# Top-32 attention and a mixture of experts on one core: the last key chunk of the outputs on 64 columns per head

## The chip, the core and the metric

The kernel runs on one core of one Trainium2 chip. The metric is device time in microseconds (us), median of the runs; a lower number is better. The core has five engines that run their own instruction streams and meet at semaphores: TensorE (PE in the profile; PEld is its weight load), VectorE (DVE), ScalarE (ACT), GpSimd (POOL) and SyncE (SP), which here starts transfers.

## What is computed

Two blocks, one after the other, all in float32. First attention in which each query keeps the 32 largest of its 576 scores. Then each of the 4608 rows goes to the one expert of eight whose gate is largest.

```python
B, H, S, D = 8, 8, 576, 64
scores = (q @ k.transpose(0, 1, 3, 2)) / sqrt(D)
kth = np.partition(scores, -32, axis=-1)[..., -32:-31]
scores = np.where(scores >= kth, scores, -1e9)
attn = softmax(scores)
x = (attn @ v).transpose(0, 2, 1, 3).reshape(4608, 512)

e = argmax(x @ w_gate, axis=1)          # 8 experts
gate = softmax(x @ w_gate)[arange, e]
y = gate[:, None] * (relu(x @ w1[e]) @ w2[e])   # 512 -> 1024 -> 512
```

The change is in `attn @ v`.

## The kernel before

**Units and groups.** Two heads of one batch element make a unit: their 64 + 64 dimensions fill the 128 partitions. There are 8 x 4 = 32 units. A unit's 576 queries are cut into four tiles of 128 for each head, and a last tile in which the 64 remaining queries of both heads lie together. Two tiles are worked at a time, a group. Two units have 9 groups, so there are 18 groups for a batch element and 144 in all.

**What happens to a group.** TensorE multiplies the scores (L276), ScalarE copies them to SBUF (L283). VectorE folds them with two-input maxima and minima (L290, L292, L298, L300) and finds the 32 largest with its max-of-8 and replace instructions (L329, L338, L345). ScalarE turns the threshold into `low` (L354) and computes how far each score lies below it (L370). GpSimd subtracts that from the scores (L379), so that the exponential on ScalarE (L387) is zero for what isn't kept. TensorE transposes the weights (L398 for four chunks of 128 keys, L409 and L411 for the last 64 keys), and ScalarE copies the transposed weights out of PSUM into `wT` (L402, L404) and `wTt` (L417, L419).

**Where the last keys lie.** 576 keys are `NC` = 4 chunks of 128 and 64 keys over. `wT` has a plane for each chunk and head. `wTt` has the last 64 keys of both heads in one: the first head's on partitions 0 to 63, the second's on 64 to 127. The values `v` are laid out to match when they are put on the device: chunk `NC` of `n.v` has the first head's last values on its first 64 partitions in columns 0 to 63, the second head's on the other 64 partitions in columns 64 to 127, and zeros elsewhere.

**Outputs.** `outputs` (L421) makes a unit's output, transposed, in two halves of `HF` = 288 queries. For each half, the four chunks are multiplied head by head: 64 columns of values, written to the head's own 64 partitions of the bank `po` (L431). The chunk with the last keys is one product for both heads, on all 128 columns (L432). ScalarE copies the bank to `oT` (L434). After the second half, `oT` is transposed back into rows and multiplied with the gate's weights in one (L443), copied (L450), and GpSimd divides by the softmax sums (L466 to L479).

**Banks.** `po`, `wTm`, `wTl`, `px` and `rank` come from one pool of two PSUM banks that take turns (`bank`, L240). A tile that is asked for waits until the copy out of the bank's last tile is done.

**Order.** Inside the loop, program order is kept on TensorE, ScalarE and VectorE (`manual_schedule`). For group `i`, `loop` (L909) issues the search of `i`, the score copies of `i + 3`, the transposes of `i - 1`, the exponentials of `i`, and the score products of `i + 4`. A unit's output is spread over the following groups by named places (`ending`, L804): a half is multiplied at the place "products", behind the score products, and copied at "relu" of a later group, ahead of the score copies.

**Expert blocks.** Rows are scattered to DRAM by expert as their batch element is done, and blocks of 128 rows of one expert are worked in pieces (L688, L703) between the attention's products on TensorE. How many pieces a group gets is counted out by a credit when the program is built (L944 to L951), so it doesn't depend on the clock. What is left runs after the attention.

Of the kernel before, what the change touches and what calls it, by code (L numbers as in the profile page):

```python
# [35 lines left out]
def kernel(  # L36
# [46 lines left out]
    nc = tc.nc  # L83
# [6 lines left out]
    NC = 4  # L90
    SM = NC * P
    ST = S - SM
    KC = NC + 1
    HF = S // 2
# [73 lines left out]
    for odd in range(2):  # L168
        for h in range(2):
            r = slice(h * D, (h + 1) * D)  # L170
# [31 lines left out]
    wT = const.tile([P, NC, 2, S + ST], F32, name="wT")  # L202
    wTt = const.tile([P, S + ST], F32, name="wTt")
# [36 lines left out]
    def bank(name):  # L240
        return k.ps_t.tile([P, SM], F32, name=name, tag="t")
# [179 lines left out]
    def outputs(n, x):  # L421

        odd = n.u % 2
        oT = oT_of[odd]
        for j in range(2):
            q = slice(j * HF + (0 if odd else ST), (j + 1) * HF + (0 if odd else ST))
            po = bank("po")
            for c in range(NC):
                for h in range(2):
                    r = slice(h * D, (h + 1) * D)  # L430
                    nc.tensor.matmul(po[r, 0:HF], n.v[:, c, r], wT[:, c, h, q], start=(c == 0), stop=False)  # L431
            nc.tensor.matmul(po[:, 0:HF], n.v[:, NC, :], wTt[:, q], start=False, stop=True)  # L432
            yield
            nc.scalar.copy(oT[:, j * HF:(j + 1) * HF], po[:, 0:HF])  # L434
            yield
        starts = [t * P + (ST if odd else 0) for t in range(NC)] + [0 if odd else SM]
        xw = P + lw
        n.xl = k.small.tile([P, KC, xw], F32, name="xl", bufs=1)
        put = []
        for t0, t1 in ((0, KC - 2), (KC - 2, KC)):  # L440
            px = bank("px")
            for t in range(t0, t1):
                nc.tensor.matmul(  # L443
                    px[:, (t - t0) * xw:(t - t0 + 1) * xw], oT[:, starts[t]:starts[t] + P],
                    turn[:, n.u // 2, odd * lw:odd * lw + xw], start=True, stop=True,
                )
            put.append((n.xl[:, t0:t1, :], px[:, 0:(t1 - t0) * xw].rearrange("p (t w) -> p t w", w=xw)))
        yield
        for to, px in put:
            nc.scalar.copy(to, px)  # L450
# [30 lines left out]
    def choice(lg):  # L481

        r = SimpleNamespace(lg=lg)
        mx = k.small.tile([P, KC], F32, name="mx")
        r.oh = oh = k.small.tile([P, KC, E], F32, name="oh")
        idx = k.small.tile([P, KC], F32, name="idx")

        def steps():
            nc.vector.tensor_reduce(mx, lg, axis=AX.X, op=ALU.max)
            yield  # L490
            nc.vector.tensor_tensor(oh, lg, _inner(mx[:, :], E), op=ALU.is_ge)
            yield
            nc.vector.tensor_tensor(oh, oh, _ins(e_less[:, :], 1, KC), op=ALU.mult)
            yield
            nc.vector.tensor_tensor(lg, lg, _inner(mx[:, :], E), op=ALU.subtract)
            yield
            nc.vector.tensor_reduce(idx, oh, axis=AX.X, op=ALU.min)
            yield
            nc.vector.tensor_tensor(oh, e_same, _inner(idx[:, :], E), op=ALU.is_equal)
            yield  # L500

        r.steps = steps()
        return r
# [231 lines left out]
    with fast:  # L735
# [68 lines left out]
        def ending(b, u):  # L804
# [3 lines left out]
            if u == 0:  # L808
                x_of[b] = k.xp.tile([P, KC, XW], F32, name="x")
                in_turn(token_ids(x_of[b][:, :, Dm + 1].bitcast(I32), b))  # L810
                lg_of[b] = k.small.tile([P, KC, E], F32, name="lg")
            x, lg = x_of[b], lg_of[b]
            out_steps = outputs(n, x)
            yield "products"
            next(out_steps)
# [191 lines left out]
    with ExitStack() as outer:  # L1007
# [10 lines left out]
        with ExitStack() as st:  # L1018
# [7 lines left out]
            with tc.For_i(0, B, 1) as b:  # L1026
# [3 lines left out]
                for u in range(0, U, 2):  # L1030
                    two = [load_unit(b, u), load_unit(b, u + 1)]
                    for n in two:
                        load_values(n)
                        open_unit(n)
                    for g in groups(u):
                        tiles = [(two[a - u], tile) for a, tile in g]
                        s, steps = scores(products(tiles))
                        for step in steps:
                            step()
                        low, nbias, _ = search(tiles, s, None)  # L1040
                        w = depths(s, low)
                        less(s, w)
                        weights(tiles, w, nbias)
                        for _ in transposed(tiles, w):
                            pass
                        n, tile = tiles[0]
                        if tile == (NC - 1 if n.u % 2 else 2 * NC):
                            for _ in outputs(n, x):
                                pass
                            for _ in divisors(n):  # L1050
                                pass
                            logits(n, lg)
                            rows(n, x)
                r = choice(lg)
# [68 lines left out]
```

## Time and profile before

| | before |
|---|---|
| time, median of 3 runs | 1380.28 us (1379.79 to 1381.28) |
| span of the profiled run | 1378.2 us |
| PE busy | 1242.7 us (90%) |
| DVE busy | 1097.6 us (80%) |
| ACT busy | 919.9 us (67%) |
| POOL busy | 649.9 us (47%) |
| L431, outputs, four chunks, 64 columns | 154.8 us, 1024 instructions |
| L432, outputs, last keys, 128 columns | 48.2 us, 128 instructions |
| L434, copies to `oT`, on ACT | 25.3 us, 64 instructions |

Busy time of an engine is time in which at least one of its instructions ran. Matmuls overlap in a pipeline, so a group's busy time is less than its instructions' durations added up, and one that starts every 0.24 us can be shown with a duration of 0.4 us. A float32 product stands in the trace as two matmul instructions.

### The profile page before, as it was taken

To read this page: it belongs to the slowest core of one execution; us is meant where nothing else is said; L and a number is where in the kernel's file an instruction comes from. 1 tells how busy PE (TensorE), PEld (TensorE's weight loads), DVE (VectorE), ACT (ScalarE), POOL (GpSimd) and SP (SyncE) were. 2 spreads that over 40 slices of the span, in tenths; PEclk is the share of its full clock that TensorE was granted. 3 is DMA by queue.
4 is the path that set the end of the run, shared out by engine and by line. 5 is a ranking of instruction groups with operands and counts; after the bars stand their busy time and mean duration, and the time that the engine had idled before them with its cause. 6 is when DMAs were issued, how large, how long until landed. Compare 5 with 4: busy or idle time off the path is not lost. (4 is left out here: it accounts for less than half of the span.)

```text
span 1378.2 us, 24231 instructions
## 1 busy us (share of the span) xinstructions
PE 1242.7 (90%) x7538; PEld 847.1 (61%) x7538; DVE 1097.6 (80%) x4655; ACT 919.9 (67%) x2049; POOL 649.9 (47%) x805
## 2 busy tenths in 40 slices
PE   5776777776799999999999999999999999999995
PEld 3444444444466666766766666767676677776773
DVE  8999999999999999999999999999999820000000
ACT  4788777777788888888777788887777821111110
POOL 3454547546645666466555565675556621000000
PEclk9878787888899999999999999999999999999998
DMA  2000011001483267327645474358552859999880
GB/s 82 29 29 29 28 36 55 29 29 36 162 295 127 106 213 277 132 78 247 246 167 173 149 274 161 109 169 302 187 174 66 315 181 354 387 319 330 302 322 18
DMA packets 102219, 231.66 MB, mean 168 GB/s; under 512 B 5182, under 2 KB 25918, under 8 KB 102080
## 3 DMA queue, kind: packets, MB, share of 16 engines
q1 hardware_dynamic: 95328, 209.76, 43.2%
q0 software_dynamic: 6464, 19.97, 4.0%
q8 instruction: 61, 1.00, 0.3%
q14 instruction: 78, 0.64, 0.1%
q10 hardware_dynamic: 288, 0.30, 0.1%
HBM read 208.72 MB, written 22.33 MB: 168 GB/s over the span
## 5 line engine op out<-in xcount | busy, mean ns | idle before, releaser
L379 POOL TENSOR_TENSOR w<-s,w 128x576 f32<-128x576 f32 x288 | 407.2, 1434 | 451.8 <-ACT w L370 451.7
L688 PE MATMUL ph<-xTs,w 128*128 128x128 f32 x2560 | 307.6, 276 | 6.0 <-ACT xTs L665 6.0
L688 PEld LDWEIGHTS ph<-xTs,w 128*128 128x128 f32 x2560 | 298.3, 192 | 23.2 <-issue 14.9
L703 PE MATMUL py<-w,hT 128*128 128x512 f32 x640 | 292.0, 596 | 0.0
L338 DVE MAX8 tops<-scr 128x8 f32<-128x168 f32 x864 | 248.3, 319 | 0.1
L276 PE MATMUL sc<-qkb 64*128 64x288 f32 (+1 forms) x1280 | 224.1, 476 | 9.6 <-ACT s L283 5.2
L387 ACT ACTIVATE w<-w,nbias 128x576 f32<-128x576 f32 x288 | 224.8, 799 | 2.7 <-POOL w L379 2.5
L370 ACT ACTIVATE w<-s,low 128x576 f32<-128x576 f32 x288 | 207.6, 768 | 4.7
L398 PE MATMUL wTm<-turn,w 128*128 128x128 f32 x1152 | 175.2, 291 | 34.5 <-ACT xl L450 21.1
L398 PEld LDWEIGHTS wTm<-turn,w 128*128 128x128 f32 x1152 | 140.2, 149 | 84.0 <-ACT xl L450 23.5
L1002 DVE CAST any_i<-pd 1x1 int32<-1x1 f32 x1 | 0.1, 146 | 236.0 <-PE pd L1000 236.0
L703 PEld LDWEIGHTS py<-w,hT 128*128 128x128 f32 x640 | 114.6, 190 | 116.9 <-issue 115.6
L345 DVE MATCH_REPLACE8 scr<-tops,scr 128x168 f32<-128x168 f32 x576 | 177.9, 314 | 0.0
L283 ACT COPY s<-sc 128x576 f32<-128x576 f32 x288 | 169.9, 645 | 11.3 <-PE sc L276 10.7
L404 ACT COPY wT<-wTm 128x512 f32<-128x512 f32 x256 | 139.9, 609 | 39.4 <-PE wTm L398 39.2
L276 PEld LDWEIGHTS sc<-qkb 64*128 64x128 f32 (+1 forms) x1280 | 119.2, 197 | 73.2 <-issue 26.0
L431 PE MATMUL po<-wT,vb 128*64 128x288 f32 x1024 | 154.8, 450 | 0.4 <-ACT wTt L419 0.4
L709 POOL DMA_INDIRECT out_dram<-y,xg x40 | 40.6, 1015 | 212.1 <-ACT y L717 199.8
L329 DVE MAX8 few<-l 128x8 f32<-128x288 f32 x288 | 128.0, 445 | 0.0
L431 PEld LDWEIGHTS po<-wT,vb 128*64 128x64 f32 x1024 | 74.7, 151 | 77.2 <-issue 26.1
L693 ACT ACTIVATE hT<-ph 128x512 f32<-128x512 f32 x80 | 48.8, 609 | 108.2 <-PE ph L688 108.1
L290 DVE TENSOR_TENSOR h<-s 128x576 f32<-128x576 f32 x144 | 112.5, 781 | 4.4 <-ACT s L283 4.4
(116 smaller groups left out, 1444.0 us busy)
## 6 DMA issues: line engine op xcount, KB each, us to landing
w<-in_moe_w_dram SPq DMA_DIRECT2D x80, 2048.0 KB, 9.8
qkb<-in_qk_dram SPq DMA_DIRECT2D x31, 608.0 KB, 4.2
xg<-x_rows SPq DMA_DIRECT2D x40, 257.0 KB, 9.8
vb<-in_v_dram SPq DMA_DIRECT2D x32, 320.0 KB, 3.2
x_rows<-blank SPq DMA_DIRECT2D x5, 257.0 KB, 13.8
x_rows<-blank POOLq DMA_DIRECT2D x4, 257.0 KB, 8.7
x_rows<-x,posi POOLq DMA_INDIRECT x40, 3.0
out_dram<-y,xg POOLq DMA_INDIRECT x40, 6.1
```

The costliest lines, as they stand in the source:

```text
L276: nc.tensor.matmul(ps[rows, j, 0:HF], n.q[d, cols], n.k[d, keys], start=True, stop=True)
L283: lambda m=m, ps=ps: nc.scalar.copy(s[:, m, :, :], ps[:, :, 0:HF]) for m, ps in enumerate(got)
L338: nc.vector.max(out=tops[:, m, r * 8:(r + 1) * 8], in_=src[m])
L345: nc.vector.match_replace(out=scr[:, m, :], in_to_replace=tops[:, m, r * 8:(r + 1) * 8], in_values=src[m], imm_value=NEG,)
L370: nc.scalar.activation(w[:, m, :], s[:, m, :, :].rearrange("p j k -> p (j k)"), AF.Relu, scale=-STEEP, bias=low[:, m:m + 1],)
L379: k.last_pool = in_turn(nc.gpsimd.tensor_tensor(w[:, m, :], s[:, m, :, :].rearrange("p j k -> p (j k)"), w[:, m, :], op=ALU.subtract)).ins
L387: nc.scalar.activation(w[:, m, :], w[:, m, :], AF.Exp, scale=scale, bias=nbias[:, m:m + 1], accum_out=n.z[:, c:c + 1])
L398: nc.tensor.transpose(pm[:, c * P:(c + 1) * P], w[:, m, first:first + P], ident)
L404: nc.scalar.copy(wT[:, :, m, q], pm4)
L431: nc.tensor.matmul(po[r, 0:HF], n.v[:, c, r], wT[:, c, h, q], start=(c == 0), stop=False)
L688: nc.tensor.matmul(ph[:, f, :], n.w1[:, 0, dt, fc * P:(fc + 1) * P], n.xT[:, dt, :], start=(dt == 0), stop=(dt == DT - 1),)
L703: nc.tensor.matmul(py, hT[:, f, :], n.w2[:, 0, f, :], start=(f == 0), stop=(f == FT - 1))
```

## The change

The last keys' product is made like the others: for each head by itself, on the head's 64 columns, with the same moving data `wTt`. The zeros in `n.v` see to it that a head takes only its own keys. So a half has five pairs of products on 64 columns and none on 128, and TensorE doesn't change between the two forms inside a half.

```diff
-            for c in range(NC):
+            for c in range(KC):
                 for h in range(2):
                     r = slice(h * D, (h + 1) * D)
-                    nc.tensor.matmul(po[r, 0:HF], n.v[:, c, r], wT[:, c, h, q], start=(c == 0), stop=False)
-            nc.tensor.matmul(po[:, 0:HF], n.v[:, NC, :], wTt[:, q], start=False, stop=True)
+                    rhs = wT[:, c, h, q] if c < NC else wTt[:, q]
+                    nc.tensor.matmul(po[r, 0:HF], n.v[:, c, r], rhs, start=(c == 0), stop=(c == KC - 1))
```

`KC` is `NC + 1` = 5.

## The prediction

> **What bounds the kernel now.** I read the page first: its slices in time show two stages.
>
> ```profile
> PE   5776777776799999999999999999999999999995
> DVE  8999999999999999999999999999999820000000
> ```
>
> A slice is 34.5 us. VectorE is full from slice 2 to 31, the attention, some 1,085 us. After it TensorE alone is full and works off the expert blocks that are left. TensorE is also full from slice 12 on, beside VectorE, so I asked for busy time by 100 us (columns: the stretch, its length, then PE, PEld, DVE, ACT, POOL busy with counts, granted clock, DMA).
>
> ```profile
> 200.00:300.00 100.00, 74.30 (x397) 45.24 (x398) 99.86 (x425) 79.60 (x181) 61.60 (x76) 0.83 0.13 41
> 500.00:600.00 100.00, 98.17 (x645) 68.26 (x644) 99.88 (x427) 83.58 (x189) 52.79 (x68) 1.00 0.60 217
> 700.00:800.00 100.00, 98.73 (x633) 68.33 (x631) 98.68 (x402) 77.14 (x173) 58.20 (x69) 1.00 0.51 181
> 1200.00:1300.00 100.00, 100.00 (x586) 73.80 (x585) 0.00 (x0) 16.50 (x28) 6.79 (x7) 1.00 0.90 321
> ```
>
> Up to 380 us TensorE has a quarter of its time free: nothing saved on it there can count. From 400 us both are full, yet VectorE does fewer instructions in 700 to 800 (402 against 427) in the same busy time. So single VectorE instructions got longer. The line that shows it is L298, a two-input maximum of 0.447 us (the line's median, which I take as undisturbed):
>
> ```profile
> 100.00:400.00 300.00, 20.62 (x41) 0.84 0.21 71
> 400.00:590.00 190.00, 13.38 (x26) 1.00 0.50 178
> 590.00:820.00 230.00, 19.09 (x29) 1.00 0.54 192
> 875.00:1095.00 220.00, 17.32 (x28) 1.00 0.52 184
> ```
>
> (VectorE time of L298 alone, with its count.) At 0.447 us, 29 would take 12.96 us; they took 19.09, an excess of 6.1 us in 590 to 820; 28 would take 12.5 us, an excess of 4.8 us in 875 to 1095. The timeline at 702 us, all engines, has the cause and a second loss:
>
> ```profile
> 701.98 1.41 POOL L379 TENSOR_TENSOR w<-s,w 128x576 f32<-128x576 f32 x1
> 702.69 1.02 DVE L298 TENSOR_TENSOR few<-h 128x288 f32<-128x288 f32 x1
> ...
> 703.80 0.89 ACT L450 COPY xl<-px 128x432 f32<-128x432 f32 x2 [2.60 <-PE px L443]
> ...
> 704.58 1.19 ACT L283 COPY s<-sc 128x576 f32<-128x576 f32 x2
> ...
> 705.74 1.26 POOL L479 TENSOR_TENSOR x<-xl,rz 128x640 f32<-128x640 f32 x1
> 705.80 1.81 DVE L290 TENSOR_TENSOR h<-s 128x576 f32<-128x576 f32 x1 [1.24 <-ACT s L283]
> ```
>
> L298 starts while GpSimd's L379 runs (to 703.39) and can't finish before that. L379 is here because ScalarE came late to L354 and L370, and ScalarE came late because it had stood waiting for TensorE. At 703.80 it had waited 2.60 us for `px`; its score copies are late by that, and VectorE stands for 1.24 us. The same happens near 987 us. So in two stretches, 590 to 820 and 875 to 1095, TensorE and ScalarE together set the pace and VectorE follows, with its lost time booked as busy. Elsewhere VectorE sets it.
>
> Last, the places the change touches: one output half in the TensorE timeline, and the waits.
>
> ```profile
> 717.39 1.38 PE L431 MATMUL po<-wT,vb 128*64 128x288 f32 x10
> 718.70 0.75 PE L432 MATMUL po<-wTt,vb 128*128 128x288 f32 x2
> 719.29 0.27 PE L398 MATMUL wTm<-turn,w 128*128 128x128 f32 x1
> ```
>
> ```profile
> ACT oT L434 <- PE po L432: 44.0, 48, 2.6
> PEld wTm L398 <- ACT oT L434: 19.5, 51, 1.6
> ```
>
> In 48 of 64 halves ScalarE stands waiting for L432, and in 51 of 64 a weight load of the next transposes waits for the copy that follows. That is because `po` and `wTm` take turns on two banks. L432 is thus in a ring that goes from TensorE to ScalarE and back.
>
> **What the Trainium skill says.** "TensorEngine Tiling (Array Packing)", Key Properties: changing the tiling mode drains TensorE, changing the tile does not. The trace agrees, and gives the size below (0.10 us). "TensorE: Matmul & The Clock Gate", Part 3, The mechanism: matmuls on different tiles run together, starting about 4 ns apart. The trace agrees: the ten instructions from 717.39 are five pairs, and a later cut of the same view starts with eight of them at 717.63, so a pair takes 0.24 us, no longer than one full-width pass. "SBUF — State Buffer", Who interferes with whom: a VectorE instruction with two SBUF inputs and a GpSimd instruction that reads SBUF exclude each other. L298 above agrees: 1.02 us beside L379 against 0.447 us.
>
> **The change part by part.** Each float32 product appears as two instructions, its passes (1024 records of L431 for 512 products). Removed: 64 full-width products L432, 128 instructions. Added: 128 products on 64 columns, 256 instructions, as 64 pairs. Weights and moving data have the sizes of L431's, and the semaphore wait for `wTt` is old: L419 was done before, since the four earlier key chunks take 2 us.
>
> *Streaming.* Two passes of L432 at 0.242 us: 0.485 us. Two passes of a pair at 0.242: 0.485 us. Difference 0.
>
> *The switch of mode.* Five pairs from 717.39 should end streaming at 717.39 + 5 x 0.242 = 718.60. L432 starts at 718.70: 0.10 us of drain. From there to L398 it takes 0.59 us where two passes need 0.485: another 0.105 us, the weight load that nothing hides. So L432 costs 0.20 us more than its streaming. With the change the fifth chunk stays in 64-column mode and starts at 718.60; the switch moves to whatever follows. There the drain is again 0.10, and the unhidden load is 0.06 us when L398 follows (its first pass takes 0.33 us after a wait, 0.27 without) and up to 0.105 us for an expert piece. On TensorE alone this gains 0 to 0.05 us a half, at most 64 x 0.05 = 3 us in the whole kernel. I take 0 where a piece follows.
>
> *What gains more is the ring.* `po` is finished 0.20 us earlier. In the half above, the oT copy L434 starts at 719.49, right after it, and the second group of transposes, whose load waited for L434, at 719.94. After the change: the pair's second pass starts at 718.85 (L432's at 719.05), L434 at 719.29, and the second group at 719.74. The first group would be through at 718.85 + 0.242 + 0.10 + 0.06 + 4 x 0.109 = 719.69, so L434 still ends the wait last, and the full 0.20 us is kept. ScalarE's score and `wT` copies behind L434 move by the same.
>
> *How many count.* From the timeline, 590 to 820 has 13 halves. Ten have ScalarE waiting for `po` and the ring closed behind it: 10 x 0.20 = 2.0 us. Two (614, 622) find ScalarE busy, and one (768) has pieces ahead of the transposes: 0. In 875 to 1095 there are nine such halves: 1.8 us. Together 3.8 us. I take four fifths, as a stretch begins and ends with groups where VectorE still sets the pace: 3.0 us.
>
> *Does VectorE follow?* At 704 and 987 us it stands and waits, so there it follows one for one until the 1.24 us are used up. Where L298 waits for the second L379, it is released when L379 ends, so that too moves one for one. What TensorE is ahead at 1095 us counts in full, since it then works until 1362 us with waits of about 3 us in all. Two halves after 1095 (1106, 1112) find ScalarE busy or are followed by L443: about 0.
>
> **Rivals.** *Hidden* (30%): VectorE is at 99.9% in most 100 us, and TensorE's time only becomes waiting. For it: ScalarE's L354 stands waiting for VectorE in 66 of 144 groups, 82.7 us in all, so ScalarE is often early. Against it: the two stretches. Then only the end's few tenths remain: 1379.9 us.
> *More than linear* (17%): the GpSimd work moves clear of VectorE's two-input instructions. At 705.74 L479 began 0.06 us before L290 and cost it 1.07 us (1.81 against 0.74); if VectorE starts first, that is gone, and both stretches look alike, so a hit that goes, goes twice. Two or three hits of 0.6 to 1.1 us, twice, on top of 3.0 us: about 1373.5 us.
> *Slower* (10%): the same shifts put L379 and L479 onto L298, L300 or L454 where they miss now. Four new hits of 0.6 to 1.2 us in each stretch are 7 us, less the 3.0: 1384.5 us. If the two columns did not overlap, the pair would take 0.97 us instead of 0.485, and 19 halves in the stretches 9 us more; the ten records from 717.39 speak against it.
> *The forecast* (43%): 1380.3 - 3.0 = 1377.3 us.
>
> **How the numbers follow.** "Faster by over 0.2%" means under 1377.5 us: the third case (17%) and some 31 of the forecast's 43 points, 48%. "Same": the other 12 and the hidden case, 42%. Slower 10%. The range leaves out the slower case and the outer part of the third: 1372.8 (3.8 us in full, some waits of 0.06 saved elsewhere, and three hits gone) to 1381.0.
>
> **What would show it.** Right: no full-width row of `po`; 1280 records on 64 columns with 288 moving; the wait of ScalarE for `po` down by 48 x 0.2, from 44 to about 35 us; L298's time in both stretches down by 1 to 2 us each; nothing changed before 380 us and after 1115 us. Wrong: a pair pitch over 0.25 us in the fifth chunk; a wait on `wTt` ahead of it; L298, L300 or L454 longer in sum than before; or the wait of L398 for L434 gone up by what the wait for `po` lost.

## The result, and the profile after

| | before | after |
|---|---|---|
| time, median of 6 runs | 1380.03 us (1379.15 to 1381.28) | 1374.71 us (1374.17 to 1377.84) |
| ratio, with its 95% interval | | 0.9964 (0.9951 to 0.9977) |
| span of the profiled run | 1378.2 us | 1372.9 us |

The change takes 5.0 us off (3.2 to 6.8 by the interval), and the kernel is faster, as forecast. The forecast of 1377.3 us was 2.6 us too high; the range of 1372.8 to 1381.0 us holds the time.

The slices of the page have the same two stages, with VectorE's last full one in the same place:

```profile
PE   5676777677899999999999999999999999999995
DVE  8999999999999999999999999999999820000000
```

The stretches of 100 us are as full as before. VectorE's counts, 433 and 398 where they were 427 and 402, can't be compared closely, since the stretches begin at another point of the work.

```profile
500.00:600.00 100.00, 98.43 (x659) 68.36 (x659) 99.88 (x433) 84.41 (x189) 53.99 (x68) 1.00 0.61 216
700.00:800.00 100.00, 98.94 (x661) 70.08 (x662) 98.63 (x398) 77.94 (x174) 59.71 (x71) 1.00 0.52 183
```

The groups of instructions, where the 128 full-width ones of L432 stood with 48.2 us, have 256 on 64 columns:

```profile
L432 PE MATMUL po<-wTt,vb 128*64 128x288 f32 x256 | 41.9, 406 | 0.0
```

Now the output half that the prediction took apart, in the TensorE timeline of the changed kernel. (In its file one line, L432, holds all the products of `po`; the moving tile tells them apart.)

```profile
713.75 2.16 PE L432 MATMUL po<-wT,vb 128*64 128x288 f32 x16
715.74 0.66 PE L432 MATMUL po<-wTt,vb 128*64 128x288 f32 x4
716.33 1.22 PE L398 MATMUL wTm<-turn,w 128*128 128x128 f32 x8
717.39 0.39 PE L688 MATMUL ph<-xTs,w 128*128 128x128 f32 x2
```

The same half in the kernel before:

```profile
715.44 1.24 PE L276 MATMUL sc<-qkb 64*128 64x288 f32 x8
716.61 2.16 PE L431 MATMUL po<-wT,vb 128*64 128x288 f32 x16
718.70 0.75 PE L432 MATMUL po<-wTt,vb 128*128 128x288 f32 x2
719.29 1.31 PE L398 MATMUL wTm<-turn,w 128*128 128x128 f32 x8
720.44 1.95 PE L688 MATMUL ph<-xTs,w 128*128 128x128 f32 x16
```

In the changed kernel the four chunks take 1.99 us to the start of the fifth (0.05 us of it the load in front of the first), so the fifth follows at the pace of the others, 8 x 0.242 us and no drain. Before, 2.09 us passed from the first chunk to the full-width product. The drain and the open load now stand at 716.33, in front of the transposes. The stretch from the first chunk to the expert piece that comes after the transposes is 717.39 - 713.75 = 3.64 us. Before it is 720.44 - 716.61 = 3.83 us. That is 0.19 us less in this half, for the 0.20 of the prediction.

The waits on both sides of the copy (total in us, times, longest):

```profile
ACT oT L434 <- PE po L432: 34.4, 42, 2.4
PEld wTm L398 <- ACT oT L434: 10.0, 27, 1.6
```

ScalarE's wait for `po` went from 44.0 to 34.4 us, as forecast (35). The transposes' wait for the copy went from 19.5 to 10.0 us. In the timelines the wait is still there in all 27 halves from 411 to 1062 us that transposes follow, but shorter: the fifth transpose pass starts 0.185 us behind the fourth (middle value) where it was 0.325 us, and 0.109 us is the pace without a wait. The room in which the change of form hides is nearly used up.

VectorE's L298 in the two full stretches (the columns as in the prediction):

```profile
590.00:820.00 230.00, 17.65 (x29) 1.00 0.54 192
...
875.00:1095.00 220.00, 16.96 (x28) 1.00 0.54 192
```

It lost 1.44 us in the first (from 19.09) and 0.36 in the second (from 17.32). And the place at which VectorE stood for 1.24 us, in its timeline:

```profile
702.94 1.80 DVE L290 TENSOR_TENSOR h<-s 128x576 f32<-128x576 f32 x1 [1.25 <-ACT s L283]
```

It still stands 1.25 us, and still loses a microsecond to L479. But it does so 2.86 us earlier than before (705.80), some 1 us of which has nothing to do with the change, as the next table shows: VectorE was ahead by then, and everything moved together.

**Where the time went, by group.** The timelines give, for each of the 144 groups, the end of its search on VectorE. This is how far it lies from the kernel before, in us:

```
end before, us      411     501     590     682     780     873     964    1062    span
after             -1.04   -1.35   -1.81   -2.34   -3.31   -4.03   -4.38   -5.36   -5.30
after, again      -0.99   -1.27   -1.72   -2.40   -3.22   -3.94   -4.45   -5.27   -5.62
```

Up to 411 us lies a piece that is no work of the change. A kernel with nothing changed in the loop (the one with the doubled memset, below) has -1.00 there, and another, changed only behind the outputs, has +0.02: single executions differ by that much up to there, so only what is gained from 411 us on counts. From 411 to 1062 us the changed kernel gains 4.32 us, and its second run 4.28, steadily, in the two stretches that the prediction had named and outside them. TensorE begins its last output half (1110.39 us before) 4.6 us ahead by the same reckoning (5.61 less 1.04) and works on with hardly a wait, 0.4 us from 1130 us on.

### The profile page after: what moved, and what is told of

It is laid out like the page before. It is cut to its first block, busy times and chain, and to the rows that moved or that the text cites. A ratio compares the mean times of both kernels' runs of the same rounds, so it can differ in the third digit from the quotient of the medians.

```text
span 1372.9 us, 24487 instructions
## 1 busy us (share of the span) xinstructions
PE 1235.4 (90%) x7666; PEld 839.2 (61%) x7666; DVE 1092.9 (80%) x4655; ACT 919.6 (67%) x2049; POOL 646.9 (47%) x805
## 5 line engine op out<-in xcount | busy, mean ns | idle before, releaser
L379 POOL TENSOR_TENSOR w<-s,w 128x576 f32<-128x576 f32 x288 | 407.4, 1435 | 449.4 <-ACT w L370 449.2
L398 PEld LDWEIGHTS wTm<-turn,w 128*128 128x128 f32 x1152 | 135.3, 148 | 96.1 <-issue 35.8
L432 PE MATMUL po<-wT,vb 128*64 128x288 f32 x1024 | 155.0, 450 | 0.4 <-ACT wTt L419 0.4
L432 PEld LDWEIGHTS po<-wT,vb 128*64 128x64 f32 x1024 | 74.7, 151 | 78.0 <-issue 28.5
L290 DVE TENSOR_TENSOR h<-s 128x576 f32<-128x576 f32 x144 | 114.9, 798 | 3.8 <-ACT s L283 3.8
```

Of the source, the lines that this page charges most:

```text
L379: k.last_pool = in_turn(nc.gpsimd.tensor_tensor(w[:, m, :], s[:, m, :, :].rearrange("p j k -> p (j k)"), w[:, m, :], op=ALU.subtract)).ins
L398: nc.tensor.transpose(pm[:, c * P:(c + 1) * P], w[:, m, first:first + P], ident)
L432: nc.tensor.matmul(po[r, 0:HF], n.v[:, c, r], rhs, start=(c == 0), stop=(c == KC - 1))
```

## The experiments

Two theories. *The ring*: what counts is when the product is done for which ScalarE stands waiting; TensorE time behind it is free as long as it lies in TensorE's own wait for ScalarE. *TensorE time*: what counts is drains and loads taken off TensorE, wherever they stand. A third, *chance*: the shift alone makes GpSimd and VectorE meet less often.

**One half at a time.** The new form for the halves with `side` true, the old for the others:

```diff
+            side = j == 0
-            for c in range(NC):
+            for c in range(KC if side else NC):
...
-            nc.tensor.matmul(po[:, 0:HF], n.v[:, NC, :], wTt[:, q], start=False, stop=True)
+            if not side:
+                nc.tensor.matmul(po[:, 0:HF], n.v[:, NC, :], wTt[:, q], start=False, stop=True)
```

> The change made in the first half of each unit alone (32 of 64), the second halves as before. Ring theory (the copies of `po` start 0.2 us earlier and TensorE, ScalarE and then VectorE follow in the full stretches): about half of the whole change's 5.3 us, 2 to 3.5 us faster than before. Theory of TensorE time (what counts is drains and loads taken off TensorE): in the same proportion. Theory of chance meetings between GpSimd and VectorE: no relation to the number of halves; anything from 3 us slower to 5 us faster.

Measured: 0.9975 of before (0.9967 to 0.9983), 3.5 us faster.

With `side = j == 1`:

> The change in the second halves alone. Ring and TensorE time: what the first halves leave, so that the two gains add up to 5.3 us within 1.5 us. The second halves of units with an odd number are sometimes followed by expert pieces and not by transposes, so they may give less than half (1.5 to 3 us). Chance: the two don't add up.

Measured: 0.9992 (0.9983 to 1.0), 1.1 us faster, and the interval touches no change. The two add up to 4.6 us of the 5.0. Reckoned from 411 to 1062 us as in the table above they gain 2.81 and 1.54 us, 4.35 us for the whole change's 4.32. (The end of this trace can't be used: TensorE's granted clock, the share of full speed that it is allowed, is 0.5 for 3.4 us in the last output half, from 1108.5 us, and its four chunks take 3.48 us for 2.09. The profiled runs of before and of the changed kernel have no such stretch there. Those with the last keys first and with the products swapped, further down, do.) From 400 to 1100 us the first halves are followed by transposes; of the second, eleven of twenty are followed by an expert piece. There the trace shows the last pass of `po` 0.197 us earlier in this kernel than before and TensorE no earlier with what follows (next start 0.094 us later, its open load 0.104): all is given back at once. That fits the ring, but the two theories forecast too nearly the same here to part them.

**More changes of form.** The kernel before with the full-width product in another place:

```diff
+            for at, c in enumerate((0, 1, NC, 2, 3)):
```

> The kernel before, with the full-width product of the last keys put between the chunks 1 and 2: the half changes form once more ahead of the copy. `po` is done some 0.15 us later than before, and one more change of form (0.16 us with a transpose behind it) comes after it. Ring: slower than before by about 0.15/0.2 of 5.3 us, 3 to 5 us. TensorE time: 0.3 us for each half more, slower by 5 to 8 us. Chance: no direction.

Measured: 1.0062 (1.0048 to 1.0076), 8.6 us slower. In its trace the last pass of `po` starts 0.151 us later than before, as forecast, and ScalarE's wait grew from 44.0:

```profile
ACT oT L437 <- PE po L435: 55.5, 54, 2.8
```

This is above what I had given the ring (3 to 5) and by the point above TensorE time too (5 to 8), into which the interval of 6.6 to 10.5 us reaches. I had left out that in the halves with a piece behind them the second change of form, 0.094 + 0.104 us, is hidden by nothing. With the rate that the pair ahead shows below (3.9 us for 0.117 us) the 0.151 us make 5.0 us, and eleven such halves 2.2 more: 7.2 us, inside the interval.

The same with the order `(NC, 0, 1, 2, 3)`:

> The kernel before, with the full-width product first and the four chunks behind it. The forms change as often ahead of the copy as before (`po` done at the same time, within 0.05 us), but one change more comes after it, ahead of what follows. Ring: the change behind the copy is hidden in the wait for the copy where transposes follow, so within 1.5 us of before (if `wTt` is there in time). TensorE time: 0.15 us more for each half, slower by 3 to 5 us.

Measured: 1.0115 (1.0099 to 1.013), 15.9 us slower, outside both. The condition about `wTt` did not hold:

```profile
ACT oT L437 <- PE po L435: 66.5, 52, 4.3
...
PEld po L431 <- ACT wTt L419: 22.0, 29, 1.3
PEld po L431 <- ACT wTt L417: 15.3, 16, 1.9
```

At the head of the half TensorE's weight load waits 37.3 us for ScalarE's copies of `wTt`, where it was 11.7 us (8.7 and 3.0) before; there the product of the last keys itself comes 2 us later, behind the other chunks. So this kernel measures a longer wait and tells nothing of the theories. It does show a cost of putting the last keys first.

**The score products behind the outputs.**

```diff
-                if i + AHEAD + 1 < len(work):
-                    multiply(i + AHEAD + 1)
...
                 at_place("products")
+                if i + AHEAD + 1 < len(work):
+                    multiply(i + AHEAD + 1)
```

> The kernel before, with the products at the place "products" (output halves, rows, ranks) issued ahead of the score products of the group and not behind them. `po` is then done 1.2 us earlier, under the score products, and ScalarE no longer stands for it. Ring: the wait of ScalarE for `po` falls from 44 us to under 15 us, and the kernel is faster by 3 to 8 us, unless the score copies, which come 2.5 us later, become the wait in its place. TensorE time: one change of form more in each half, so 0 to 5 us slower.

> The changed kernel with the same swap. Ring: the 0.2 us ahead of the copy are hidden under the score products now, so the change brings less here than without the swap (0 to 3 us between this and the swap of before). TensorE time: the change now takes a whole change of form away (0.2 us on TensorE in each half), so it brings 5 us or more. If the swap works as the ring theory says, this is the fastest of the four.

Measured: 0.9986 (0.9978 to 0.9994) without the change and 0.9948 (0.9934 to 0.9961) with it. The change is worth 5.2 us here too, where I had given the ring 0 to 3 and TensorE time 5 or more. The swap alone is 1.9 us faster. I had given the ring 3 to 8 us, unless the score copies become the wait, and TensorE time 0 to 5 us slower, so here TensorE time missed. The waits of the first of the two show why the ring's forecasts were wrong:

```profile
ACT s L283 <- PE sc L276: 45.5, 64, 3.5
...
ACT oT L434 <- PE po L432: 6.4, 8, 4.3
```

ScalarE no longer stands for `po`, but it stands 45.5 us for the score products, which are behind `po` now. The ring wasn't opened; it closes one product later. With the change the same two lines are:

```profile
ACT s L283 <- PE sc L276: 34.4, 58, 3.4
...
ACT oT L434 <- PE po L432: 5.2, 5, 4.1
```

11.1 us less, 0.17 us in each of 64 halves. So this pair doesn't part the theories, and it widened the first one: it is not `po` that counts but whatever ScalarE stands waiting for.

**Chance.** One memset on VectorE doubled at the start:

```diff
     nc.vector.memset(turn, 0.0)
+    nc.vector.memset(turn, 0.0)
```

> The kernel before, with one memset on VectorE doubled at the start, which moves the engines against each other by a fraction of a microsecond and touches nothing in the loop. Chance: the time moves by 2 us or more either way. Ring and TensorE time: within 1 us of before.

Measured: 1.0005 (0.9997 to 1.0013). But the trace shows that nothing was shifted. The second memset ran at 1.54 us while VectorE stood waiting for a transfer, and it went on at 5.20 us, for 5.18 before: the memset took 0.33 us from that wait. So this is a repeat of before and no test of *chance*. What speaks against *chance* is that the gains of the two sets of halves add up (4.35 for 4.32 us), and that the two profiled runs of the changed kernel, which lie up to 0.7 us apart in their first 400 us, gain 4.32 and 4.28 us.

**The same dose ahead of the copy and behind it.** These part the first two theories. Ahead: a short pair of products, which the first chunk overwrites.

```diff
             po = bank("po")
+            for h in range(2):
+                r = slice(h * D, (h + 1) * D)
+                nc.tensor.matmul(po[r, 0:D], n.v[:, 0, r], wT[:, 0, h, q][:, 0:D], start=True, stop=True)
```

> The kernel before, with a short pair of products on 64 columns (64 queries, written over by the first chunk) put ahead of each output half: about 0.12 us more on TensorE ahead of `po` in each of 64 halves, no further change of form. If it is the time at which `po` is done that counts: 40 halves from 400 to 1100 us times 0.12 us, slower than before by 3 to 5 us. TensorE time: the same.

Measured: 1.0028 (1.0016 to 1.0041), 3.9 us slower. One half in its TensorE timeline, the added pair second:

```profile
717.25 1.24 PE L276 MATMUL sc<-qkb 64*128 64x288 f32 x8
718.42 0.34 PE L430 MATMUL po<-wT,vb 128*64 128x64 f32 x4
718.59 2.11 PE L434 MATMUL po<-wT,vb 128*64 128x288 f32 x16
720.63 0.75 PE L435 MATMUL po<-wTt,vb 128*128 128x288 f32 x2
```

From the score products to the full-width product it is 3.38 us, where the half of before that began at 715.44 took 718.70 - 715.44 = 3.26: a dose of 0.12 us (0.117 in the median of the trace).

Behind: the first transpose pass doubled in the group that follows an output half, where no piece comes between. `k.behind` is set after L432 and cleared by a piece.

```diff
-            for c in range(NC):
+            for c in ([0] if k.behind and not m else []) + list(range(NC)):
```

> The kernel before, with one transpose pass doubled (0.11 us on TensorE) behind those output halves that the transposes follow at once: it lies in the wait for the copy to `oT`, which has some 0.2 us of room. If it is the time at which `po` is done that counts: within 1 us of before. TensorE time: slower by 29/40 of what the pair ahead costs at the same dose, 2 to 4 us.

Measured: 1.0 (0.9992 to 1.0009). Its timeline at the same half:

```profile
719.56 0.75 PE L434 MATMUL po<-wTt,vb 128*128 128x288 f32 x2
720.15 1.31 PE L400 MATMUL wTm<-turn,w 128*128 128x128 f32 x9
721.30 0.39 PE L691 MATMUL ph<-xTs,w 128*128 128x128 f32 x2
```

Nine transpose passes take from 720.15 to 721.30, 1.15 us. Before, eight took from 719.29 to 720.44, 1.15 us: the ninth ran in the wait. The trace has 52 added passes of 0.11 us, 5.7 us of TensorE time that cost nothing to the interval's 1.2 us, while the pair ahead cost 3.9 us for 64 x 0.117 = 7.5 us. Only doses from 400 us on, where TensorE is full, can be compared: 29 passes, 3.2 us, for nothing and 40 pairs, 4.7 us, for 3.9 us. At the rate of the pair the passes would have cost 2.6 us, over twice what the interval leaves. That is the ring, and it rules out TensorE time.

By group, as in the table above, these kernels show when it happens:

```
end before, us      411     501     590     682     780     873     964    1062    span
pair ahead        -0.43    0.53    1.22    1.74    2.27    2.70    3.38    3.90    4.60
pass behind        0.02    0.87    0.88    0.86    0.86    0.82    0.86    0.86    0.97
memset doubled    -1.00   -0.84   -0.81   -0.87   -0.87   -0.87   -0.86   -0.88   -0.67
```

From 411 to 1062 us there are 38 halves, 4.45 us of the dose ahead, and the kernel loses 4.33 us. The first 90 us are not safe to read, though: there the pass behind loses 0.85 us too, and not again afterwards, and the cause of that is open. From 501 us on the pair ahead loses 3.37 us for 32 x 0.117 = 3.74, the pass behind and the memset nothing (within 0.05). So nine tenths of what is put ahead of `po` comes out on VectorE, and over the whole time, not in two stretches.

**Both together.** The swap with the change was the fastest kernel, so it ran once more beside the changed kernel alone.

> The changed kernel once more, beside the others: 0.9964 of before within the interval.

> The changed kernel with the products at the place "products" ahead of the score products once more, on the same chip as the changed kernel alone: 1 to 3 us faster than that one, if the earlier difference (0.9948 against 0.9964 of before) was one.

Measured: 0.9965 (0.9951 to 0.9978) and 0.9943 (0.9929 to 0.9956); medians 1375.7 and 1373.48 us. The swap adds some 2 us in both sets (1374.7 and 1373.3 in the first), and in the second set, where both ran, each of its runs is faster than each of the change alone (up to 1373.98 against 1374.04 and more). The intervals against before overlap a little, so that it is faster than the change alone is likely and not shown beyond doubt. Against before it is faster by 7.2 and 7.9 us.

## Why the prediction was right, and where its sum was off

*Streaming* and *the switch of mode*: right to the hundredth. (The two products of a pair start 7 ns apart in both traces; the 4 ns that the prediction quotes are not what this kernel shows.) In the trace the last pass of `po` starts 0.197 us earlier (0.20 said). What follows starts 0.094 us later behind it (0.10), with 0.055 us of open load for a transpose and 0.104 for a piece (0.06 and 0.105).

*The ring*: right, and shown by the doses ahead and behind. The working of the one half came within 0.01 us (0.19 of 0.20). That the score and `wT` copies move along is shown indirectly, by the score products' wait in the swapped kernels and by the score products that come 0.19 us earlier (next).

*How many count*: this is the term that was mis-sized. It took ten and nine halves in two stretches, since elsewhere "VectorE sets it", and four fifths of those: 3.0 us. By the table the change gains 4.3 us from 411 to 1062 us. Some 3.3 of that lie in the two stretches (of the 3.8 counted, so four fifths was a little low), and 1.0 outside, where none was counted: 0.77 us from 411 to 590 and the rest between the stretches. The timelines say which halves count, if one takes the time from a half's first pass to the score products that follow. Of the 37 halves that begin from 411 to 1062 us it is 0.18 to 0.19 us shorter in 26: seventeen in the two stretches (in the first they are just the ten that the prediction counted) and nine outside. In the others it isn't: the copy starts no earlier, as ScalarE isn't waiting for `po`, or a piece that follows takes the gain back. The first halves alone show the rule: fifteen of eighteen pass on 0.187 us and three (476, 610, 891 us), where ScalarE doesn't stand waiting for `po`, nothing. 15 x 0.187 = 2.8 us, and VectorE gains 2.81 us. That the runs' median says 5.0 and the trace 4.3 is inside the interval.

I had read VectorE at 99.88% busy in 500 to 600 us as proof that it sets the pace. It isn't. VectorE's idle time from 411 to 1062 us is 3.3 us in both kernels, the same to 0.02 us, so its whole gain of 4.32 us is in instructions that got shorter: L300 by 2.4 us and L298 by 1.4, some small ones of the row placement by 2.1, with L290 longer by 1.4 and L454 by 0.3. In the second run of the changed kernel the parts differ (L298 by 2.7, L300 by 0.1) and the sum is 4.28 again. VectorE follows while it looks full: instructions such as L298 beside L379 hold waits in their own busy time.

*Does VectorE follow?*: yes, but not as told. The 1.24 us at 704 us were not used up. What the table shows is that it follows over the whole time, by 0.3 to 1.0 us in each twelve groups.

*Rivals.* Hidden: ruled out by the result and by the pair ahead. More than linear: the measured time is nearer to it (1373.5) than to the forecast, and single hits did go, since L300 takes 2.4 us less from 411 to 1062 us. But others came (L290 takes 1.4 us more, and L479 still hits it at 702.94), the second run has other parts and the same sum, and the gain goes by the number of halves. So the hits are where the gain shows; that they are its source isn't what the runs suggest. Slower: one new hit of 0.8 us shows near 1081 us in both profiles of the changed kernel, and the gain is larger.

*What would show it.* No full-width row, as said, and ScalarE's wait at 34.4 for 35 us. L298 fell by 1.44 us in the first stretch, as forecast, and by only 0.36 in the second. One of the signs of being wrong did show: L454 takes 14.8 us in all, for 13.4 before. L298 and L300 fell in sum (80.3 to 78.5 and 69.4 to 67.5 us), so that sign alone told nothing of the time. That nothing changes before 380 us can't be read from the profile of before, which was late by nearly 1 us for its own reasons.

## What to carry to other kernels

When two engines pass work to and fro, look for the product at which the other stands: here a delay ahead of it came out to nine tenths, and one behind it not at all while it lay in the wait for the answer. So a cost that can't be removed, such as TensorE's change between column forms, may still be moved behind the hand-over. A small dose put in at each place is a cheap way to tell the two apart, once the trace shows that the dose isn't swallowed by a wait of its own, as the memset's was; and a busy share of 99% doesn't say that an engine sets the pace if its busy time can hold waits.

## What the runs showed that I had not expected

VectorE, 98.6 to 99.9% busy in each 100 us from 400 to 1000 us, passes on 3.37 of 3.74 us of delay that was put on TensorE. "Perfetto Trace Analysis", Identifying the Most-Contended Engine, in the Trainium skill finds the bottleneck by occupancy and calls it, for VectorE, also a fair measure of how close one is to the limit; here VectorE's occupancy says neither. Taking away ScalarE's wait for one product (the swap) gave it back as a wait for the next, nearly whole: 37.6 us less for `po` (44.0 to 6.4), 34.8 us more for the score products (10.7 to 45.5).
